# Decode attention with a gated MLP on one core: three adjoining slabs, wq in one transfer, wo in fewer, x and gate turned on VectorE

## The chip, the core and the metric

The kernel runs on one core of a Trainium2 chip. A core has a matrix engine (TensorE, "PE" in the profile, its weight loads "PEld"), VectorE ("DVE"), ScalarE ("ACT"), GpSimd ("POOL") and SyncE ("SP"), which here does nothing but issue transfers from the chip's memory into the on-chip buffer and back. The engines run side by side and wait for one another through semaphores. 16 DMA engines carry the transfers. The metric is the device time of one execution in microseconds; the kernel before takes 696.23 us (median of 3 runs, 696.22 to 696.31).

## The reference

Two tokens (batch B = 2, one position) of width 640. One branch is an attention block over a cache of 4096 positions with 32 heads of 128, the other a small MLP; a sigmoid gate mixes them.

```
g = sigmoid((x * gate_w).sum(-1, keepdims=True))            # x: (2, 1, 640)
q = (x @ wq).reshape(B, 1, 32, 128).transpose(0, 2, 1, 3)   # wq: (640, 4096)
scores = einsum("bhqd,bhkd->bhqk", q, k_cache) * 128 ** -0.5
o = einsum("bhqk,bhkd->bhqd", softmax(scores), v_cache)     # caches: (2, 32, 4096, 128)
a = o.transpose(0, 2, 1, 3).reshape(B, 1, 4096) @ wo        # wo: (4096, 640)
b = silu(x @ w1) @ w2                                       # w1: (640, 1728), w2: (1728, 640)
out = g * a + (1 - g) * b
```

All is float32. The two caches are 268 MB of the 298 MB that are read; wq and wo are 10.5 MB each, w1 and w2 4.4 MB each.

## The kernel before

**Tiling.** An item is four heads of one batch row; there are 16 (`items`, N = 16). For one item K is one contiguous run of 8.4 MB, loaded as 128 partitions of 16384 elements into a slab, and V likewise. There are three slabs, `slab_a`, `slab_b` and `slab_v`: K alternates between a and b, V uses v, except V of the last item, which goes into a.

**One item.** TensorE spreads the item's query over the partitions (`query`), GpSimd and VectorE multiply K by it (`products`), VectorE sums over 128 elements (`scores`) and finds the maximum (`peak`), ScalarE takes the exponentials (`weights`), TensorE multiplies them with V (`values`, 32 matmuls at L759), VectorE scales (`combine`), TensorE gathers (`gather`) and VectorE turns the result into columns of `oP` (`turn`).

**What sets the order.** The program is recorded once, operation by operation, in `Flow`: every `f.op` and `f.dma` names what it reads and writes, and `plan` works out the waits. Each engine then runs its list in the order of recording. All loads are issued by SP in order, so a load that waits holds up every load behind it in SP's list. Once issued, transfers of the one queue follow one another on the DMA engines. A slab's next load waits for the users of the slab: K of item i + 2 for `scores` of item i, V of item i + 1 for `values` of item i.

**The start.** SP issues w1 (into part of slab v), x (two rows) and gate (one row) beside it, wq in two pieces (8.4 MB into slab a, 2.1 MB into slab v), w2 into slab b, and a first write of zeros to the output. TensorE turns x and gate with matmuls against the identity (`mm_xT`), VectorE copies them (`xz`, `gx`), and the gate's sum goes through TensorE, ScalarE and VectorE to g and 1 - g (`gc`). `mm_qr` forms the queries of all heads in two PSUM banks, its first 32 matmuls from slab a, its last 8 from slab v; the load of the first K into slab a stands between them in the recording. ScalarE copies the queries out (`copy_qr`); a shifted identity brings the second batch row to where the first stood. `mm_hr` forms the hidden layer of the MLP from w1, VectorE rearranges it (`spaced`, `turned`, `he`, `seq`), and `ffn_out` (L587) multiplies by w2. The first V waits for `mm_hr`, the second K for `ffn_out`.

**The end.** After the last V, wo is loaded in four groups of 1024 rows (2.6 MB each; `load_wo`). Groups 0 and 1 are one transfer each and group 2 is two, all into slab v once the V before the last has been used; group 3 is three transfers of 5, 2 and 1 rows per partition into slab b. `in_halves` (L610) multiplies groups 0 to 2, eight steps each with two matmuls a step; for groups 0 and 1 the steps alternate between two halves of the output bank, for group 2 they stay in one. `merge` copies the bank and folds it with four matmuls (L627), `in_quarters` (L640) adds group 3 with four matmuls a step, VectorE copies the result, and SP sends it.

Of the kernel before, what the change touches and what calls it, by code (L numbers as in the profile page):

```python
# [16 lines left out]
class Flow:  # L17
# [22 lines left out]
    def op(self, eng, fn, reads=(), writes=(), by=(), signal=None, loop=None, after=(), lower=()):  # L40
        deps = list(after)
        for r in reads:
            if r in self.writer:
                deps.append(self.writer[r])
            if r.startswith("ps_"):
                deps += [d for d in self.readers.get(r, ()) if d.eng != eng]
        for w in writes:
            if w in self.writer:
                deps.append(self.writer[w])
            deps += self.readers.get(w, ())  # L50
        o = Op(eng, fn, deps, by, signal, loop)
        o.dma, o.lower = False, lower
        o.idx = len(self.ops[eng])
        self.ops[eng].append(o)
# [19 lines left out]
    def plan(self):  # L74
        seen = {e: {} for e in self.engines}
        for o in self.all:
# [88 lines left out]
def gated_decode(nc, x, kc, vc, wq, wo, w1, w2, gate, out):  # L165
    P = 128
# [46 lines left out]
    IW = 160  # L213
    ident_w = sb("ident", [P, IW])
    ident = ident_w[:, :P]
    ones = sb("ones", [P, P])
    fold = sb("fold", [P, 2 * Q, Q, 4])
    sel = sb("sel", [P, 4 * Q])
# [6 lines left out]
    g = sb("g", [P, B])  # L225
    gc = sb("gc", [P, B])
    ge = sb("ge", [P, B])
    gx = sb("gx", [P, B, J])
# [60 lines left out]
    def load_wo(g):  # L289

        n, at = ("v", g * PD) if g < NP - 1 else ("b", 0)
        src = wo[g * PR * P : (g + 1) * PR * P, :].rearrange("(p n) d -> p (n d)", n=PR)
        cuts = (0, PD) if g < NP - 2 else (0, PD // 2, PD) if g < NP - 1 else (0, FIRST * D, PD - D, PD)
        after = f.users(part(n)) if g in (0, NP - 1) else wo_after
        for k, (c0, c1) in enumerate(zip(cuts, cuts[1:])):
            f.dma("SP", slab[n][:, at + c0 : at + c1], src[:, c0:c1], writes=part(n, g % (NP - 1) + k), after=after)
        return after

    wq_rows = wq.rearrange("(p j) n -> p (j n)", j=J)
    f.dma(
        "SP",
        slab["v"][:, W1_AT : W1_AT + J * F],
        w1.rearrange("(p j) f -> p (j f)", j=J),
        writes=part("v", 1, 2, 3, 4, 5),
    )
    xg = slab["v"][: B + 1, XG_AT : XG_AT + D]
    f.dma("SP", xg[:B], x.rearrange("b s d -> (b s) d"), writes=part("v", 6))
    f.dma("SP", xg[B : B + 1], gate[None, :], writes=part("v", 7))  # L310
    f.dma("SP", slab["a"], wq_rows[:, :SLAB], writes=part("a"))
    f.dma("SP", slab["v"][:, :W1_AT], wq_rows[:, SLAB:], writes=part("v", 0))
    f.dma(
        "SP",
        slab["b"][:, : FH * HD],
        w2.rearrange("(p r) (e c) -> p (r e c)", p=P // 2, e=2).rearrange("p (e c) -> (p e) c", e=2),
        writes=part("b"),
    )

    f.op("POOL", lambda: G_.memset(ident_w, 0.0), writes=["ident"])  # L320
    f.op(
        "POOL",
        lambda: G_.affine_select(
# [15 lines left out]
    for q in range(Q):  # L339
# [38 lines left out]
        reads=["ident"],  # L378
        writes=["side"],
    )  # L380
    for q in range(Q):
        f.op(
            "DVE",
            lambda q=q: V.tensor_copy(
                spread[:, q * QP : (q + 1) * QP], ident[:, 32 * q : 32 * q + 1].to_broadcast([P, QP])
            ),
            reads=["ident"],
            writes=[f"spread{q}"],
        )
    SPREAD = [f"spread{q}" for q in range(Q)]  # L390
# [18 lines left out]

    def mm_xT():
        for j in range(J):
            last = T_.matmul(
                ps_v[:, j * (B + 1) : (j + 1) * (B + 1)],
                xg[:, j:D:J],
                ident[: B + 1, : B + 1],
                start=True,
                stop=True,
            )  # L420
        return last

    f.op("PE", mm_xT, reads=part("v", 6, 7) + ["ident"], writes=["ps_v"])
    xT = ps_v[:, : J * (B + 1)].rearrange("p (j r) -> p j r", j=J)
    f.op("DVE", lambda: V.tensor_copy(xz[:, :, :B], xT[:, :, :B]), reads=["ps_v"], writes=["xz"])
    for b in range(B):
        f.op(
            "DVE",
            lambda b=b: V.tensor_mul(gx[:, b, :], xT[:, :, B], xz[:, :, b]),
            reads=["ps_v", "xz"],  # L430
            writes=[f"gx{b}"],
        )
    f.op("DVE", lambda: V.reduce_sum(gp, gx, axis=AX.X), reads=["gx0", "gx1"], writes=["gp"])
    f.op(
        "PE",
        lambda: T_.matmul(ps_o[:, :B], ones, gp, start=True, stop=True),
# [15 lines left out]
    qr = (ps_0, ps_1)  # L452
    HALF = HQ // 2

    def mm_qr(j0, j1):
        for j in range(j0, j1):
            t, k = (slab["a"], j) if j < J0 else (slab["v"], j - J0)
            w = t[:, k * H * DH : (k + 1) * H * DH].rearrange("p (h q d) -> p h q d", q=Q, d=DH)
# [11 lines left out]
    f.op("PE", lambda: mm_qr(0, J0), reads=part("a") + ["xz"], writes=["ps_0", "ps_1"])  # L470
    load_k(0)
    f.op("PE", lambda: mm_qr(J0, J), reads=part("v", 0) + ["xz"], writes=["ps_0", "ps_1"])

    def copy_qr(u, b):
        return S_.copy(qall[:, u * HALF : (u + 1) * HALF, b, :], qr[u].rearrange("p (h d) -> p h d", d=DH))

    for u in range(2):
        f.op("ACT", lambda u=u: copy_qr(u, 0), reads=[f"ps_{u}"], writes=[f"qall{u}0"])

    def mm_query(i):  # L480
        return T_.matmul(  # L481
# [22 lines left out]

    query(0)
    copy_q(0)
    for u in range(2):
        f.op(
            "PE",
            lambda u=u: T_.matmul(  # L510
                qr[u],
                ident_w[:, 1 : P + 1],
                qall[:, u * HALF : (u + 1) * HALF, 0, :],
                start=True,
                stop=True,
            ),
            reads=["ident", f"qall{u}0"],
            writes=[f"ps_{u}"],
        )
        f.op("ACT", lambda u=u: copy_qr(u, 1), reads=[f"ps_{u}"], writes=[f"qall{u}1"])  # L520

    rows = ps_v
    w1t = slab["v"][:, W1_AT : W1_AT + J * F].rearrange("p (j f) -> p j f", j=J)

    def mm_hr():
        for j in range(J):
            for c in range(Q):
                last = T_.matmul(  # L530
                    rows[32 * c : 32 * c + 32, :QF],
                    xz[:, j, :],
                    w1t[:, j, c * QF : (c + 1) * QF],
                    start=(j == 0),
                    stop=(j == J - 1),
                )
        return last

    f.op("PE", mm_hr, reads=part("v", 1, 2, 3, 4, 5) + ["xz"], writes=["ps_v"])


    tv = turned[:, : 32 * FR].rearrange("p (n r) -> p n r", r=32)
    h = tv[:, :, :B]
    pairs = rows[:, :QF].rearrange("p (m s) -> p s m", s=FH)
    for e in range(2):
        f.op(
# [22 lines left out]
            writes=[f"seq{e}"],  # L569
        )  # L570

    load_v(0)

# [5 lines left out]
    def ffn_out(n):  # L579
# [13 lines left out]
                )  # L593
            return last

        f.op("PE", fn, reads=["seq0", "seq1"] + part(n), writes=["ps_acc"])

    def heads(g):
        return [f"oP{g}{u}{b}" for u in range(2) for b in range(B)]
# [1 line left out]
    def in_halves(g):  # L601

        for k in range(PR):
# [12 lines left out]
                    )  # L616
                return last

            f.op("PE", fn, reads=part("v", g + (g == NP - 2 and k >= PR // 2)) + heads(g), writes=["ps_acc"])

    def merge():
        f.op("ACT", lambda: S_.copy(partial, early), reads=["ps_acc"], writes=["partial"])
# [223 lines left out]
    for i in range(N + 1):  # L846
# [20 lines left out]
            peak(i)  # L867
            weights(i)
        if i == N - 1:
            wo_after = None  # L870
            for g_ in range(NP):
                wo_after = load_wo(g_)
        if j >= 0:
            combine(j)
            gather(j, by=by("combine"), loop=loop)
# [71 lines left out]
```

## Time and profile before

| | |
|---|---|
| median of 3 runs | 696.23 us (696.22 to 696.31) |
| profiled execution | 696.23 us |
| its span in the profile | 694.9 us |
| bytes read | 298.26 MB |
| DVE busy | 488.7 us (70% of the span) |
| POOL busy | 266.0 us (38%) |
| PE busy | 219.6 us (32%) |
| granted TensorE clock, mean | 0.67 |

How to read the profile's lines. A timeline row is: start in us, duration, engine, source line, operation, output<-input, shape, how many instructions were merged into the row, and in brackets how long the engine had been idle before it and what ended that idle time. A row of the chain gives start, duration and what ran. A row of groups gives count, busy time, mean ns of one, and the idle time before with what ended it. A row of transfers gives the count, the size and the time from issue to landing. A row of windows gives the stretch, its length, the busy time of each engine in it (PE, PEld, DVE, ACT, POOL, each with its number of instructions), the granted TensorE clock, the share of the DMA engines and the rate in GB/s; asked for PE alone, it has the columns of PE only. "SPq" is SyncE issuing a transfer. TensorE leaves two records for one float32 matmul.

### The profile page before, as it was taken

The page shows a single profiled execution, that of the slowest core. Times are in us where ns is not written, and L with a number is a line of the kernel's source. Part 1 is how long each engine was busy: PE and PEld are TensorE (multiplying, and loading weights), DVE is VectorE, ACT ScalarE, POOL GpSimd, SP SyncE. Part 2 cuts the span into 40 slices and gives each one's busy share as a digit, 9 for nine tenths or more (in the row PEclk, how much of TensorE's full clock was granted, in tenths as well). Part 3 has the DMA queues.
Part 4 walks back from the last instruction along what each step waited for, and adds up shares of the span by engine and source line. Part 5 has one row for each costly group of instructions (what it writes and reads, how often), then busy time and mean ns, then how long its engine had stood idle before and what let it go on. Part 6 is the DMA issues. An engine that isn't in the chain of part 4 may idle for free. (4 is left out here: it accounts for less than half of the span.)

```text
span 694.9 us, 3685 instructions
## 1 busy us (share of the span) xinstructions
PE 219.6 (32%) x1478; PEld 73.6 (11%) x1478; DVE 488.7 (70%) x263; ACT 41.2 (6%) x153; POOL 266.0 (38%) x26
## 2 busy tenths in 40 slices
PE   1095032151331406060412405060503214050657
PEld 1022010010110102020100101010101001010113
DVE  2001958898989596886959595987869595978811
ACT  0010010101010102010010101010010101010100
POOL 1000808191826080816335170907244260908100
PEclk9998556565575757575665757575665757575789
DMA  9999999999999999999999999999999999999997
GB/s 378 427 458 438 438 423 426 426 456 438 423 430 426 453 438 426 430 423 456 434 430 430 423 453 438 430 430 423 449 438 434 430 423 434 449 438 426 426 417 310
DMA packets 6229, 298.37 MB, mean 429 GB/s; under 512 B 699, under 2 KB 715, under 8 KB 974
## 3 DMA queue, kind: packets, MB, share of 16 engines
q1 hardware_dynamic: 6222, 298.28, 99.3%
q8 instruction: 4, 0.07, 0.0%
q14 instruction: 3, 0.02, 0.0%
HBM read 298.26 MB, written 0.01 MB: 429 GB/s over the span
## 5 line engine op out<-in xcount | busy, mean ns | idle before, releaser
L759 PE MATMUL ps<-slab_v,pz 128*32 128x512 f32 x960 | 139.3, 745 | 334.4 <-PEq L151 334.4
L663 POOL TENSOR_TENSOR slab_a<-slab_a,qsb 128x7680 f32<-128x7680 f32 x8 | 131.5, 16436 | 207.0 <-DMA slab_a<-in_A_k_cache_dram 191.9
L663 POOL TENSOR_TENSOR slab_b<-slab_b,qsb 128x7680 f32<-128x7680 f32 x8 | 131.4, 16428 | 171.4 <-DMA slab_b<-in_A_k_cache_dram 155.5
L679 DVE TENSOR_REDUCE s<-slab_a 128x68 f32<-128x8704 f32 (+1 forms) x16 | 138.2, 8676 | 0.0
L679 DVE TENSOR_REDUCE s<-slab_b 128x68 f32<-128x8704 f32 (+1 forms) x16 | 138.2, 8676 | 0.0
L669 DVE TENSOR_TENSOR slab_b<-slab_b,ps 128x8704 f32<-128x8704 f32 x8 | 73.8, 9219 | 48.0 <-DMA slab_b<-in_A_k_cache_dram 48.0
L669 DVE TENSOR_TENSOR slab_a<-slab_a,ps 128x8704 f32<-128x8704 f32 x8 | 73.8, 9219 | 43.5 <-DMA slab_a<-in_A_k_cache_dram 43.5
L759 PEld LDWEIGHTS ps<-slab_v,pz 128*32 128x32 f32 x960 | 37.7, 133 | 423.6 <-issue 423.6
L708 ACT ACTIVATE pz<-s,nb 32x128 f32<-32x128 f32 x64 | 25.5, 398 | 563.9 <-PE ps L759 361.5
L797 PE MATMUL ps<-osb,pick 128*128 128x512 f32 x32 | 20.4, 724 | 60.8 <-PEq L151 59.8
L781 DVE SCALAR_TENSOR_TENSOR osb<-ps,rg,own 128x512 f32<-128x512 f32 x16 | 12.0, 749 | 23.9 <-PE ps L759 23.9
L811 DVE TENSOR_REDUCE row<-ps 64x128 f32<-64x512 f32 x16 | 10.9, 683 | 23.3 <-PE ps L797 23.3
L548 DVE COPY spaced<-ps 128x224 f32<-128x224 f32 x2 | 0.7, 386 | 33.1 <-PE ps L530 33.1
L481 PE MATMUL ps<-qall,spread 128*128 (+1 forms) x32 | 7.4, 319 | 31.8 <-PEq L151 31.1
L461 PE MATMUL ps<-slab_a,xz 128*32 128x512 f32 x64 | 9.3, 747 | 16.1 <-DMA slab_a<-in_A_wq_dram 16.1
L797 PEld LDWEIGHTS ps<-osb,pick 128*128 128x128 f32 x32 | 5.4, 211 | 74.8 <-issue 73.0
L708 ACT ACTIVATION_READ_ACCUMULATOR pz<-s,nb 32x1 f32 x64 | 11.8, 184 | 0.0
L481 PEld LDWEIGHTS ps<-qall,spread 128*128 128x128 f32 x32 | 6.7, 224 | 41.9 <-issue 40.3
L759 PE MATMUL ps<-slab_a,pz 128*32 128x512 f32 x64 | 8.4, 687 | 7.1 <-DMA slab_a<-in_A_v_cache_dram 7.1
L818 DVE STREAM_TRANSPOSE ps<-row 64x256 f32<-64x256 f32 x16 | 10.3, 643 | 0.6
L587 PE MATMUL ps<-slab_b,seq 128*32 128x320 f32 x54 | 9.4, 505 | 3.0 <-DVE seq L565 3.0
L610 PE MATMUL ps<-slab_v,oP 128*32 128x320 f32 x96 | 9.2, 434 | 1.6 <-DMA slab_v<-in_A_wo_dram 1.6
(70 smaller groups left out, 92.0 us busy)
## 6 DMA issues: line engine op xcount, KB each, us to landing
slab_v<-in_A_wo_dram SPq DMA_DIRECT2D x2, 2560.0 KB, 18.5
slab_v<-in_B_w_dram SPq DMA_DIRECT2D x1, 4320.0 KB, 14.0
slab_b<-in_B_w_dram SPq DMA_DIRECT2D x1, 4320.0 KB, 46.3
slab_v<-in_A_wo_dram SPq DMA_DIRECT2D x2, 1280.0 KB, 25.9
slab_v<-in_A_wq_dram SPq DMA_DIRECT2D x1, 2048.0 KB, 36.6
slab_b<-in_A_wo_dram SPq DMA_DIRECT2D x1, 1600.0 KB, 30.5
slab_b<-in_A_wo_dram SPq DMA_DIRECT2D x1, 640.0 KB, 31.6
slab_b<-in_A_wo_dram SPq DMA_DIRECT2D x1, 320.0 KB, 31.9
```

What stands on the lines that cost most here:

```text
L461: last = T_.matmul(qr[u][32 * q : 32 * q + 32, :], xz[:, j, :], w[:, u * HALF : (u + 1) * HALF, q, :], start=(j == 0), stop=(j == J - 1),)
L481: return T_.matmul(ps_q[:, :DH], spread, qall.rearrange("p h b d -> p (h b) d")[:, i, :], start=True, stop=True,)
L587: last = T_.matmul(early[to : to + 32, :], seq[:, k : k + 2, :].rearrange("p k z -> p (k z)"), slab[n][:, k * HD : (k + 1) * HD], start=(k ...
L663: lambda: G_.tensor_mul(k[:, CV:, :], k[:, CV:, :], qsb[:, None, :].to_broadcast([P, C - CV, DH])),
L669: lambda: V.tensor_mul(k[:, :CV, :], k[:, :CV, :], ps_q[:, None, :DH].to_broadcast([P, CV, DH])),
L679: lambda c0=c0, c1=c1: V.reduce_sum(Ss[i % 2][:, c0:c1], k[:, c0:c1, :], axis=AX.X),
L708: last = S_.activation(pz[lo:hi, :, 4 * q : 4 * q + 4], s[lo:hi].rearrange("p (g c) -> p g c", c=4), AF.Exp, bias=nb[lo:hi], scale=SCALE, ...
L759: last = T_.matmul(ps_v[32 * q : 32 * q + 32, :], pz[:, gr, :], v[:, gr, :], start=(gr < 4), stop=(gr >= NG - 4),)
L781: lambda: V.scalar_tensor_tensor(osb, ps_v.rearrange("p (c d) -> p c d", d=DH), rg, own[:, :, None].to_broadcast([P, 4, DH]), op0=ALU.mult ...
L797: lambda *_: T_.matmul(ps_o, pick, osb.rearrange("p c d -> p (c d)"), start=True, stop=True),
L811: lambda: V.reduce_sum(row, ps_o[:64].rearrange("p (c d) -> p d c", d=DH), axis=AX.X),
L818: lambda: V.transpose(oT.rearrange("p n (e i) -> p n e i", e=2), twice),
```

## The change

- The three slabs become one tensor `slabs` with three adjoining parts, in the order v, b, a. wq (20480 elements per partition) is one transfer that covers slab b and the end of slab v; `mm_qr` is one run of 40 matmuls. w1 moves to slab a and w2 to the start of slab v.
- The load of the first K into slab a is recorded after `mm_hr`, which now comes before `mm_qr`. The first V is recorded after `ffn_out`, whose weights lie in slab v.
- x and gate are loaded as twelve pieces of 160 elements onto partitions of a zeroed tile `xs` (8 of x, 4 of gate), and VectorE turns them in 32 x 32 blocks; `mm_xT` goes away.
- The queries are copied out by VectorE with a 0/1 mask per batch row (four operations), in place of ScalarE's four copies and the shifted identity's two matmuls. `spread` is built by memsets.
- wo: groups 0 and 1 in one transfer, group 2 in one. Group 3 stays at three.
- `plan` sorts the waits by the order of recording.

```diff
-            for d in sorted(o.deps, key=lambda d: -d.idx):
+            for d in sorted(o.deps, key=lambda d: -d.turn):
...
-    slab = {n: sb(f"slab_{n}", [P, SLAB], 512) for n in "abv"}
+    slabs = sb("slabs", [P, 3 * SLAB], 512)
+    slab = {n: slabs[:, k * SLAB : (k + 1) * SLAB] for k, n in enumerate("vba")}
...
+    xs = turned[:, : D // Q]
+    xt = sb("xt", [P, J, 32])
+    mask = sb("mask", [P, B])
...
-    J0 = SLAB // (H * DH)
-    W1_AT = (J - J0) * H * DH
-    XG_AT = W1_AT + J * F
+    WQ_AT = 2 * SLAB - J * H * DH
...
         n, at = ("v", g * PD) if g < NP - 1 else ("b", 0)
+        if g == 0:
+            src = wo[: 2 * PR * P, :].rearrange("(g p n) d -> p g (n d)", g=2, n=PR)
+            to = slab["v"][:, : 2 * PD].rearrange("p (g c) -> p g c", g=2)
+            f.dma("SP", to, src, writes=part("v", 0, 1), after=v_users)
+            return
+        if g == 1:
+            return
         src = wo[g * PR * P : (g + 1) * PR * P, :].rearrange("(p n) d -> p (n d)", n=PR)
-        cuts = (0, PD) if g < NP - 2 else (0, PD // 2, PD) if g < NP - 1 else (0, FIRST * D, PD - D, PD)
-        after = f.users(part(n)) if g in (0, NP - 1) else wo_after
+        cuts = (0, PD) if g < NP - 1 else (0, FIRST * D, PD - D, PD)
+        after = f.users(part(n)) if g == NP - 1 else v_users
...
+    f.op("POOL", lambda: G_.memset(xs, 0.0), writes=["xs"])
+    f.dma("SP", slab["a"][:, : J * F], w1.rearrange("(p j) f -> p (j f)", j=J), writes=part("a"))
+    f.dma("SP", xs[0:P:HB, :], x.rearrange("b s (c n) -> (s c) b n", c=Q), reads=["xs"], writes=["xs0"])
+    f.dma("SP", xs[HB // 2 : P : 32, :], gate.rearrange("(c n) -> c n", c=Q), reads=["xs"], writes=["xs1"])
+    f.dma("SP", slabs[:, WQ_AT : 2 * SLAB], wq.rearrange("(p j) n -> p (j n)", j=J), writes=part("v", 1) + part("b"))
     f.dma(
         "SP",
-        slab["b"][:, : FH * HD],
+        slab["v"][:, : FH * HD],
         w2.rearrange("(p r) (e c) -> p (r e c)", p=P // 2, e=2).rearrange("p (e c) -> (p e) c", e=2),
-        writes=part("b"),
+        writes=part("v", 0),
     )
...
+        lambda: V.transpose(xt, xs.rearrange("p (n j) -> p j n", j=J)),
+        reads=["xs0", "xs1"],
...
+    f.op("PE", mm_hr, reads=part("a") + ["xz"], writes=["ps_v"])
+
+
+    load_k(0)
...
+    f.op("PE", mm_qr, reads=part("v", 1) + part("b") + ["xz"], writes=["ps_0", "ps_1"])
+    for u in range(2):
+        for b in range(B):
+            f.op(
+                "DVE",
+                lambda u=u, b=b: V.tensor_scalar(
+                    qall[:, u * HALF : (u + 1) * HALF, b, :],
+                    qr[u].rearrange("p (h d) -> p h d", d=DH),
+                    mask[:, b : b + 1],
+                    None,
+                    op0=ALU.mult,
+                ),
...
-            f.op("PE", fn, reads=part("v", g + (g == NP - 2 and k >= PR // 2)) + heads(g), writes=["ps_acc"])
+            f.op("PE", fn, reads=part("v", g) + heads(g), writes=["ps_acc"])
...
-    ffn_out("b")
+    ffn_out("v")
+    load_v(0)
     load_k(1)
```

On SP, the end of the list before (the transfers of wo, right after the last V's):

```order
L68 DMA slab_v<-in_A_wo_dram 128x5120 [waits done_PE]
L68 DMA slab_v<-in_A_wo_dram 128x5120
L68 DMA slab_v<-in_A_wo_dram 128x2560 x2
L68 DMA slab_b<-in_A_wo_dram 128x3200 [waits done_DVE]
L68 DMA slab_b<-in_A_wo_dram 128x1280
L68 DMA slab_b<-in_A_wo_dram 128x640
```

and after:

```order
L69 DMA slabs<-in_A_wo_dram 128x2x5120 [waits done_PE]
L69 DMA slabs<-in_A_wo_dram 128x5120
L69 DMA slabs<-in_A_wo_dram 128x3200 [waits done_DVE]
L69 DMA slabs<-in_A_wo_dram 128x1280
L69 DMA slabs<-in_A_wo_dram 128x640
```

Seven transfers become five; the last three are as they were.

On PE, the start of the list before:

```order
L414 MATMUL ps<-ident,slab_v 128x3 x5
L436 MATMUL ps<-gp,ones 128x2
L461 MATMUL ps<-slab_a,xz 32x512 x32
L461 MATMUL ps<-slab_v,xz 32x512 x8
L481 MATMUL ps<-qall,spread 128x128
...
L510 MATMUL ps<-qall,ident 128x512 x2
L530 MATMUL ps<-slab_v,xz 32x432 x20
L587 MATMUL ps<-slab_b,seq 32x320 x27
```

and after:

```order
L436 MATMUL ps<-slabs,xz 32x432 x20
L451 MATMUL ps<-gp,ones 128x2
L476 MATMUL ps<-slabs,xz 32x512 x40
L502 MATMUL ps<-qall,spread 128x128
L572 MATMUL ps<-slabs,seq 32x320 x27
```

The MLP's first matmuls (L530 before, L436 after) moved ahead of the queries' (L461 before, L476 after), and the five of `mm_xT` and two of the shifted identity are gone.

More of the change, by code (lines that the diff above doesn't have):

```diff
@@ L53, in op @@
         o.idx = len(self.ops[eng])
+        o.turn = len(self.all)
         self.ops[eng].append(o)
@@ L320, in gated_decode @@
-    f.op("POOL", lambda: G_.memset(ident_w, 0.0), writes=["ident"])
+        slab["v"][:, : FH * HD],
+        w2.rearrange("(p r) (e c) -> p (r e c)", p=P // 2, e=2).rearrange("p (e c) -> (p e) c", e=2),
+        writes=part("v", 0),
+    )
+    f.op("POOL", lambda: G_.memset(ident, 0.0), writes=["ident"])
     f.op(
@@ L380, in gated_decode @@
     )
+    f.op("DVE", lambda: V.memset(spread, 0.0), writes=["spread"])
     for q in range(Q):
@@ L453, in gated_decode, with mm_qr @@
     HALF = HQ // 2
[L455 to L458, printed above, removed]
+    def mm_qr():
+        for j in range(J):
+            at = WQ_AT + j * H * DH
+            w = slabs[:, at : at + H * DH].rearrange("p (h q d) -> p h q d", q=Q, d=DH)
             for u in range(2):
@@ L468, in mm_qr @@
         return last
[L470 to L475, printed above, removed]
-    for u in range(2):
-        f.op("ACT", lambda u=u: copy_qr(u, 0), reads=[f"ps_{u}"], writes=[f"qall{u}0"])
+    f.op("PE", mm_qr, reads=part("v", 1) + part("b") + ["xz"], writes=["ps_0", "ps_1"])
+    for u in range(2):
+        for b in range(B):
+            f.op(
+                "DVE",
+                lambda u=u, b=b: V.tensor_scalar(
[5 more added lines that the diff above has]
+                ),
+                reads=[f"ps_{u}", "mask"],
+                writes=[f"qall{u}{b}"],
+            )
     def mm_query(i):
@@ L506, in gated_decode @@
     copy_q(0)
[L507 to L539, printed above, removed]
     tv = turned[:, : 32 * FR].rearrange("p (n r) -> p n r", r=32)
-    h = tv[:, :, :B]
+    h = tv[:, :, ::HB]
     pairs = rows[:, :QF].rearrange("p (m s) -> p s m", s=FH)
@@ L570, in gated_decode @@
         )
-    load_v(0)
     def ffn_out(n):
```

81 lines of the change are left out of this document (35 added, 46 removed).

## The prediction

> **What bounds the kernel now.** I read the page from the top: shares of the engines, the slices, the queues; then the chain that ended last; then the timeline of the first 70 and the last 20 us, since the change edits only these two.
>
> ```profile
> PE 219.6 (32%) x1478; PEld 73.6 (11%) x1478; DVE 488.7 (70%) x263; ACT 41.2 (6%) x153; POOL 266.0 (38%) x26
> DMA  9999999999999999999999999999999999999997
> q1 hardware_dynamic: 6222, 298.28, 99.3%
> HBM read 298.26 MB, written 0.01 MB: 429 GB/s over the span
> ```
>
> No compute engine is near full, and the one DMA queue fills 99.3% of the span (690.0 of 694.9 us). The change moves the same bytes, so what it can win is what lies outside that 99.3%: 4.9 us, at the two ends. What it can lose is larger: any moment at which the queue runs dry, and any compute that is put behind the last transfer. The chain says what stands there today.
>
> ```profile
> 659.47 30.55 DMA slab_b<-in_A_wo_dram
> 690.02 0.14 issue
> 690.15 2.16 PE ps L640 x56
> ...
> 692.34 0.51 PE ps L640 x8
> ...
> 692.88 0.33 DVE slab_v L884
> ```
>
> The end is a transfer (the first piece of wo's fourth group, group 3 in the code), then the 32 matmuls of `in_quarters` on it, the copy, and the output's transfer up to 694.9. The profiled execution took 696.23 us, 1.33 outside its span, and is equal to the median of the three runs, so the sum below is made on 696.23 directly. The timeline shows what the tensor engine does before that.
>
> ```profile
> 677.76 4.51 PE L610 MATMUL ps<-slab_v,oP 128*32 128x320 f32 x64
> 683.23 2.35 PE L610 MATMUL ps<-slab_v,oP 128*32 128x320 f32 x16 [0.95 <-DMA slab_v<-in_A_wo_dram]
> 686.27 2.35 PE L610 MATMUL ps<-slab_v,oP 128*32 128x320 f32 x16 [0.69 <-DMA slab_v<-in_A_wo_dram]
> 688.66 0.42 ACT L622 COPY slab_v<-ps 128x320 f32<-128x320 f32 x1 [28.92 <-PE ps L610]
> 689.14 0.47 PE L627 MATMUL ps<-slab_v,join 128*17 128x160 f32 x8 [0.53 <-ACT slab_v L622]
> 690.15 2.66 PE L640 MATMUL ps<-slab_b,oP 128*17 128x160 f32 x64 [0.55 <-DMA slab_b<-in_A_wo_dram]
> ```
>
> Each matmul leaves two records. Groups 0 and 1 (four blocks of output rows) take 4.51 us for 64 records; group 2 (two blocks) takes 2.35 us for 16, twice, and its first half is done while the second half is still on its way. That overlap is what one transfer for group 2 takes away.
>
> **The tail, the term that I expect to decide.** On SP and PE the third group becomes one piece. PE before:
>
> ```order
> L610 MATMUL ps<-slab_v,oP 32x320 [waits load_434]
> L610 MATMUL ps<-slab_v,oP 32x320 x15
> L610 MATMUL ps<-slab_v,oP 32x320 [waits load_435]
> L610 MATMUL ps<-slab_v,oP 32x320 x7
> L610 MATMUL ps<-slab_v,oP 32x320 [waits load_436]
> L610 MATMUL ps<-slab_v,oP 32x320 x7
> ```
>
> PE after, same place (the end of the output projection; load_431 is groups 0 and 1, load_432 group 2, load_433 the first piece of group 3):
>
> ```order
> L595 MATMUL ps<-slabs,oP 32x320 [waits load_431]
> L595 MATMUL ps<-slabs,oP 32x320 x31
> L595 MATMUL ps<-slabs,oP 32x320 [waits load_432]
> L595 MATMUL ps<-slabs,oP 32x320 x15
> L612 MATMUL ps<-slabs,join 17x160 [waits done_ACT]
> L612 MATMUL ps<-slabs,join 17x160 x3
> L625 MATMUL ps<-slabs,oP 17x160 [waits load_433,done_DVE]
> ```
>
> All 16 matmuls of group 2 now stand behind the landing that the second eight waited for, and groups 0 and 1 behind the landing of group 1. The latter is hidden: the burst from 677.76 met no wait at its middle, so group 1 had landed by 680.0, and 4.51 us from there end at 684.5, before group 2 lands. For group 2 I need the pace inside a burst and the pace of the quarters:
>
> ```profile
> 687.64 0.12 PEld L610 LDWEIGHTS ps<-slab_v,oP 128*32 128x32 f32 x2 [0.15 <-issue]
> 687.91 0.12 PEld L610 LDWEIGHTS ps<-slab_v,oP 128*32 128x32 f32 x2 [0.15 <-issue]
> 690.12 1.25 PEld L640 LDWEIGHTS ps<-slab_b,oP 128*17 128x17 f32 x40 [0.85 <-issue]
> 691.57 0.40 PEld L640 LDWEIGHTS ps<-slab_b,oP 128*17 128x17 f32 x16 [0.20 <-DMA slab_b<-in_A_wo_dram]
> 692.34 0.13 PEld L640 LDWEIGHTS ps<-slab_b,oP 128*17 128x17 f32 x8 [0.36 <-DMA slab_b<-in_A_wo_dram]
> ```
>
> A pair of records follows the next after 0.27 us, so 8 more matmuls cost 8 x 0.27 = 2.16 and the burst 2.35 + 2.16 = 4.51 us (at most 2 x 2.35 = 4.70). It starts at 686.2 and ends at 690.7. The copy and the join follow as now: join starts 689.14 - 688.62 = 0.52 later, at 691.2, its own weights take about 0.13, so the quarters can issue from 691.35, at the latest after the join's 0.47, from 691.7. By then their data has landed but for the last pieces. Eight steps at 1.25/5 = 0.25 are 2.0, and the last record ends 692.85 - 692.47 = 0.38 behind the last weights: end between 693.7 and 694.1, against 692.85 now. Today the quarters wait for their pieces (the 0.20 and 0.36 above); then those waits are gone and PE itself is late. The term is +0.85 to +1.25; I take +0.9, near the lower end, since a weight load overlaps the matmul ahead of it in every row above.
>
> **What fewer transfers save.** The last three transfers tell a transfer's own cost.
>
> ```profile
> slab_b<-in_A_wo_dram SPq DMA_DIRECT2D x1, 1600.0 KB, 30.5
> slab_b<-in_A_wo_dram SPq DMA_DIRECT2D x1, 640.0 KB, 31.6
> slab_b<-in_A_wo_dram SPq DMA_DIRECT2D x1, 320.0 KB, 31.9
> 659.47 1.38 SPq L68 DMA_DIRECT2D slab_b<-in_A_wo_dram  x3
> ```
>
> They are issued 0.46 us apart, so 640 KB land 1.56 us after the first, and 320 KB 0.76 us later: twice 0.76 less 1.56 leaves -0.04 for a fixed cost, with rounding -0.2 to +0.2. Three transfers fewer (wq 1, wo 2) save between -0.6 and +0.6; I take 0, as calculated. The 640-byte pieces of x and gate carry 7.5 KB as before and lie inside w1's and wq's time; 0.
>
> The Trainium skill (DMA: Bandwidth & Descriptors, Rules for kernel authors) says to coalesce many small transfers, and its section on the anatomy of one DMA gives a fixed cost of about 2 us each on another issuing path; by that, an estimate of 3 x 2 = 6 us would be saved. The rows above do not agree: queued transfers hide it.
>
> **The start.** SP before, then after:
>
> ```order
> L68 DMA slab_a<-in_A_wq_dram 128x16384
> L68 DMA slab_v<-in_A_wq_dram 128x4096
> L68 DMA slab_b<-in_B_w_dram 128x8640
> L68 DMA out_dram<-oP 4x2x160 [waits done_POOL]
> L68 DMA slab_a<-in_A_k_cache_dram 128x16384 [waits done_PE,load_4]
> L68 DMA slab_v<-in_A_v_cache_dram 128x16384 [waits done_PE]
> L68 DMA slab_b<-in_A_k_cache_dram 128x16384 [waits done_PE]
> ```
>
> ```order
> L69 DMA slabs<-in_A_wq_dram 128x2x10240
> L69 DMA slabs<-in_B_w_dram 128x8640
> L69 DMA out_dram<-oP 4x2x160 [waits done_POOL]
> L69 DMA slabs<-in_A_k_cache_dram 128x16384 [waits done_PE]
> L69 DMA slabs<-in_A_v_cache_dram 128x16384 [waits done_PE]
> L69 DMA slabs<-in_A_k_cache_dram 128x16384
> ```
>
> The first K now waits only for the MLP's first matmuls (it can be issued well before 43.52, and queues behind w2 all the same: 0). The first V moves the other way: w2 lies in the v slab, so V waits for `ffn_out`, and `ffn_out` now stands behind all of wq and behind four masked copies on VectorE.
>
> ```profile
> slab_v<-in_A_wq_dram SPq DMA_DIRECT2D x1, 2048.0 KB, 36.6
> 2.24 0.53 SPq L68 DMA_DIRECT2D slab_v<-in_A_wq_dram  x1
> 34.06:45.11 11.05, 11.04 (x80) 2.73 (x80) 0.00 (x0) 0.00 (x0) 0.00 (x0) 1.00 1.04 447
> 51.86 0.69 DVE L548 COPY spaced<-ps 128x224 f32<-128x224 f32 x2 [33.11 <-PE ps L530]
> 54.78 9.42 PE L587 MATMUL ps<-slab_b,seq 128*32 128x320 f32 x54 [2.99 <-DVE seq L565]
> L781 DVE SCALAR_TENSOR_TENSOR osb<-ps,rg,own 128x512 f32<-128x512 f32 x16 | 12.0, 749 | 23.9 <-PE ps L759 23.9
> 43.52 0.33 SPq L68 DMA_DIRECT2D slab_a<-in_A_k_cache_dram  x1
> 51.85 0.33 SPq L68 DMA_DIRECT2D slab_v<-in_A_v_cache_dram  x1
> slab_a<-in_A_k_cache_dram SPq DMA_DIRECT2D x1, 24.8
> 693.23 0.55 SPq L68 DMA_DIRECT2D out_dram<-slab_v  x1
> ```
>
> wq has landed at 2.24 + 36.6 = 38.84. Its 40 matmuls took 11.05 us (some of it early, on the first piece; now all of it after): 50.0. The four copies have no row; one lies between 0.35 (224 elements, L548) and 0.75 (512 elements with more operands, L781); I take 0.65, nearer the one of equal size: 52.6. From the spacing copies to `ffn_out` 54.78 - 51.86 = 2.92: 55.5. `ffn_out` 9.42: V is issued at about 65.0 instead of 51.85 (63.8 to 65.4 with the copies' bounds). The first K lands at 43.52 + 24.8 = 68.3; from an issue to the end of a small transfer it is at most 694.9 - 693.23 = 1.7, so V must be issued by 66.6. Margin 1.6 us: I cost it at 0, but the cover is thin, and was 14.7 us. The second K follows at once and has a whole V in hand (8.4 MB at 429 GB/s, 19.5 us). Every other edit of the start (the POOL memset ahead of x, x's turn and the gate on VectorE, the four matmuls and two ACT copies gone) lies under the transfers from w1 to the first K: 0. The points where the repeated and prefetched parts of the instruction lists are cut move by a few operations; VectorE waited 43.5 us for the K slabs of one of the two buffers alone, which covers it:
>
> ```profile
> L669 DVE TENSOR_TENSOR slab_a<-slab_a,ps 128x8704 f32<-128x8704 f32 x8 | 73.8, 9219 | 43.5 <-DMA slab_a<-in_A_k_cache_dram 43.5
> ```
>
> Sum: 696.23 + 0.9 + 0 + 0 = 697.1 us, 0.13% slower, which is inside the 0.2% (1.4 us) that a measurement of this kernel can about tell from no change.
>
> **Rivals.** First, slower: the clock falls in the tail. It fell once after a pause:
>
> ```profile
> 54.78:55.96 1.18, 1.18 (x8) 0.49 (x10) 0.00 (x0) 0.00 (x0) 0.00 (x0) 0.90 0.77 333
> 55.96:59.37 3.41, 3.41 (x16) 1.24 (x14) 0.00 (x0) 0.00 (x0) 0.00 (x0) 0.54 1.06 461
> ```
>
> The burst came after 2.99 us without work, and 1.2 us into it the granted clock went to 0.54 for 3.41 us. In the new tail PE pauses from 684.5 at the latest to 686.2, about 2 us, where it now pauses 0.95 and 0.69. If the clock falls there, 3.41 us run at half speed and cost 1.7: 698.8. Against it: the pause is shorter than the one that did it.
>
> The Trainium skill (TensorE: Matmul & The Clock Gate, Why this matters for your kernels) warns only of idle gaps over about 3 us; by it the sum stays as it is, and the trace's one drop agrees.
>
> Second, slower: V is issued later than 66.6. One more stretch of 3.41 us at half clock in wq's burst or in `ffn_out` costs 1.7, and the upper bound of the copies 0.4: V at 67.1, the queue stands still for 0.5, 697.6; a second such stretch makes it 699.3. It decides from 67.1 on. For it speaks that both bursts now begin after a longer pause than before.
>
> Third, no loss in the tail: the 16 DMA engines do not end together.
>
> ```profile
> 689.50:690.00 0.50, 0.10 (x4) 0.00 (x0) 0.00 (x0) 0.00 (x0) 0.00 (x0) 1.00 0.89 358
> 690.00:690.50 0.50, 0.35 (x12) 0.37 (x16) 0.00 (x0) 0.00 (x0) 0.00 (x0) 1.00 0.36 143
> ```
>
> From 690.0 only a third is busy: a few late engines set each landing. If the late ones are less late after the change, group 2 lands up to about 1.5 us sooner and all follows: 697.1 - 0.9 = 696.2 with a typical part of it.
>
> Fourth, faster: each transfer has a cost that the last pieces hide. At the 0.76 us of the whole smallest piece, three of them are 2.3: 697.1 - 2.3 = 694.8. This is the coalescing rule of the Trainium skill (DMA: Bandwidth & Descriptors, Rules for kernel authors) at a price from this trace.
>
> **Numbers.** Forecast 0.60, clock 0.13, late V 0.12, no loss 0.11, transfers' cost 0.04. Slower by over 0.2% is above 697.62: the clock (0.13), three quarters of the late V (0.09) and a tenth of the forecast (0.06): 0.28. Faster, below 694.84: most of the fourth, a little of the third: 0.04. The rest, 0.68, is no change. The range from 696.2 (third rival) to 698.5 (between the two prices of the late V, short of the clock's 698.8) leaves out 0.13 for the clock and a few hundredths each of the late V and the fourth, about 0.2.
>
> **What would show it.** Right: one burst of 32 records at L595 of about 4.5 us that starts near 686 and waits for wo; L625 without waits for its pieces, ending 0.8 to 1.2 us later than now; V's issue near 65; the queue still at 99%. Wrong: a granted clock near 0.5 after 684; no packets around 67 to 69; the first product on a K slab, right after the first K's landing, moved; or a middle of the run in which slabs wait differently.

## The result

The changed kernel takes 699.13 us (median of 6 runs, 698.76 to 699.43) against 696.23 us: a ratio of 1.0041, 95% interval 1.0031 to 1.0052. That is slower by 2.9 us; forecast were 697.1 and a range up to 698.5.

| | before | after |
|---|---|---|
| median | 696.23 us | 699.13 us |
| profiled execution | 696.23 us | 698.83 us |
| its span | 694.9 us | 696.6 us |
| spans of the other runs | 694.4 to 695.3 us (18 runs beside the first experiments) | 696.5 to 697.2 us |
| time outside the span (time less span, median over runs) | 1.34 us | 2.25 us |

Two things moved: the span by about 1.95 us (696.85 in the median of the runs, against 694.9) and the time outside it by 0.91. The queue is still full on the page of the profile after:

```profile
DMA  9999999999999999999999999999999999999996
q1 hardware_dynamic: 6060, 298.27, 99.1%
```

The chain that ended last, however, is another one.

```profile
659.39 27.35 DMA slabs<-in_A_wo_dram
...
686.79 4.53 PE ps L595 x32
...
691.34 0.43 ACT slabs L607
...
691.82 0.47 PE ps L612 x8
692.28 2.22 PE ps L625 x64
...
694.52 0.33 DVE slabs L870
```

It no longer ends in the transfer of the fourth group of wo but in that of the third: the burst of 32 records, the copy, the join and the quarters stand behind it one after the other. From that landing to the last matmul are 694.50 - 686.79 = 7.71 us; before they were 692.85 - 686.27 = 6.58. The burst also starts 0.52 us later than the second half of that group did (686.27).

The start, by the timeline of after:

```profile
38.87 11.09 PE L476 MATMUL ps<-slabs,xz 128*32 128x512 f32 x80 [17.13 <-DMA slabs<-in_A_wq_dram]
50.04 2.72 DVE L490 TENSOR_SCALAR qall<-ps,mask 128x512 f32<-128x512 f32 x4 [27.49 <-PE ps L476]
55.63 10.18 PE L572 MATMUL ps<-slabs,seq 128*32 128x320 f32 x54 [4.30 <-DVE seq L551]
65.84 0.33 SPq L69 DMA_DIRECT2D slabs<-in_A_v_cache_dram  x1
```

GpSimd's first product on a slab starts as soon as that K has landed, so its rows date the landings of the first and the second K. Before:

```profile
68.43 16.43 POOL L663 TENSOR_TENSOR slab_a<-slab_a,qsb 128x7680 f32<-128x7680 f32 x1 [64.57 <-DMA slab_a<-in_A_k_cache_dram]
107.27 16.42 POOL L663 TENSOR_TENSOR slab_b<-slab_b,qsb 128x7680 f32<-128x7680 f32 x1 [22.41 <-DMA slab_b<-in_A_k_cache_dram]
```

After:

```profile
68.49 16.43 POOL L649 TENSOR_TENSOR slabs<-slabs,qsb 128x7680 f32<-128x7680 f32 x1 [64.48 <-DMA slabs<-in_A_k_cache_dram]
108.44 16.44 POOL L649 TENSOR_TENSOR slabs<-slabs,qsb 128x7680 f32<-128x7680 f32 x1 [23.52 <-DMA slabs<-in_A_k_cache_dram]
```

The first K is on time, the second 1.17 us late: the loss lies between them, where the first V is transferred. The windows show it; before, then after. The last two columns are the DMA share and the rate; a packet counts in full in the window in which it starts, so a share can exceed 1. A row of K or V, 64 KB, is one packet.

```profile
63.90:65.75 1.85, 0.30 (x2) 0.00 (x0) 0.00 (x0) 0.00 (x0) 0.00 (x0) 1.00 1.23 531
65.75:66.75 1.00, 0.00 (x0) 0.00 (x0) 0.00 (x0) 0.00 (x0) 0.00 (x0) 1.00 1.37 590
66.75:68.25 1.50, 0.00 (x0) 0.00 (x0) 0.00 (x0) 0.00 (x0) 0.00 (x0) 1.00 0.71 306
68.25:69.75 1.50, 0.00 (x0) 0.00 (x0) 1.37 (x1) 0.00 (x0) 1.32 (x1) 0.87 1.31 568
```

```profile
63.90:65.75 1.85, 1.85 (x14) 0.56 (x8) 0.00 (x0) 0.00 (x0) 0.00 (x0) 1.00 1.31 567
65.75:66.75 1.00, 0.06 (x1) 0.00 (x0) 0.00 (x0) 0.00 (x0) 0.00 (x0) 1.00 0.00 0
66.75:68.25 1.50, 0.00 (x0) 0.00 (x0) 0.00 (x0) 0.00 (x0) 0.00 (x0) 1.00 2.01 699
68.25:69.75 1.50, 0.00 (x0) 0.00 (x0) 1.38 (x1) 0.00 (x0) 1.26 (x1) 1.00 0.00 0
69.75:71.25 1.50, 0.00 (x0) 0.00 (x0) 1.50 (x1) 0.00 (x0) 1.50 (x1) 0.87 1.61 699
```

Before, the engines took up new rows all along. After, they took up K's last sixteen rows from 63.9 us on, at 2.4 us a row (1.31 x 1.85), so the first of them were free from about 66.3; but not one row started between 65.75 and 66.75. Then V's first sixteen rows started (699 GB/s over 1.5 us are 1.05 MB), and they took 3.0 us each on average (2.01 x 1.5), where the next sixteen took 2.4 (1.61 x 1.5). So the engines that were free first stood still for some 0.4 us, and the slower first rows added 0.6: an estimate of 1.0 of the 1.17 us.

Last, what the DMA engines do at the very end (694 to 700 us). After, a transfer of the kind that the profile calls "instruction" stands there, behind the span's end (an instruction load, for short):

```profile
q14 instruction: 1, 0.01, 0.5%
q1 hardware_dynamic: 12, 0.01, 0.3%
```

Before, only the output:

```profile
q1 hardware_dynamic: 12, 0.01, 0.3%
```

So there were three candidates: the late V, the longer chain at the end, and something outside the span. The experiments take them one at a time, first by undoing each in the changed kernel, then by putting each alone into the kernel before.

### The profile page after: what moved, and what is told of

It reads as the page before. It is cut to its first block, busy times and chain, and to the rows that moved or that the text cites. A ratio compares the mean times of both kernels' runs of the same rounds, so it can differ in the third digit from the quotient of the medians.

```text
span 696.6 us, 3657 instructions
## 1 busy us (share of the span) xinstructions
PE 215.6 (31%) x1464; PEld 71.1 (10%) x1464; DVE 492.1 (71%) x269; ACT 39.0 (6%) x149; POOL 266.4 (38%) x27
## 5 line engine op out<-in xcount | busy, mean ns | idle before, releaser
L649 POOL TENSOR_TENSOR slabs<-slabs,qsb 128x7680 f32<-128x7680 f32 x16 | 263.2, 16448 | 379.2 <-DMA slabs<-in_A_k_cache_dram 348.2
L665 DVE TENSOR_REDUCE s<-slabs 128x68 f32<-128x8704 f32 (+1 forms) x32 | 276.3, 8676 | 0.0
L745 PE MATMUL ps<-slabs,pz 128*32 128x512 f32 x1024 | 145.8, 733 | 341.8 <-PEq L152 334.8
L655 DVE TENSOR_TENSOR slabs<-slabs,ps 128x8704 f32<-128x8704 f32 x16 | 147.5, 9219 | 93.4 <-DMA slabs<-in_A_k_cache_dram 93.4
L745 PEld LDWEIGHTS ps<-slabs,pz 128*32 128x32 f32 x1024 | 39.6, 132 | 434.8 <-issue 427.7
L476 PE MATMUL ps<-slabs,xz 128*32 128x512 f32 x80 | 11.1, 720 | 17.1 <-DMA slabs<-in_A_wq_dram 17.1
L572 PE MATMUL ps<-slabs,seq 128*32 128x320 f32 x54 | 10.2, 539 | 4.3 <-DVE seq L551 4.3
L436 PE MATMUL ps<-slabs,xz 128*32 128x432 f32 x40 | 5.8, 749 | 15.6 <-DVE xz L422 15.6
L595 PE MATMUL ps<-slabs,oP 128*32 128x320 f32 x96 | 9.0, 434 | 3.1 <-DMA slabs<-in_A_wo_dram 3.1
L719 PE MATMUL ps<-rs,fold 128*128 128x1 f32 x32 | 6.1, 260 | 3.5 <-PEq L152 3.4
```

The source lines that it names most:

```text
L476: last = T_.matmul(qr[u][32 * q : 32 * q + 32, :], xz[:, j, :], w[:, u * HALF : (u + 1) * HALF, q, :], start=(j == 0), stop=(j == J - 1),)
L595: last = T_.matmul(early[to + 32 * n : to + 32 * n + 32, :], oP[:, at : at + 32], slab["v"][:, s_ * D + n * W2 : s_ * D + (n + 1) * W2], s ...
L649: lambda: G_.tensor_mul(k[:, CV:, :], k[:, CV:, :], qsb[:, None, :].to_broadcast([P, C - CV, DH])),
L655: lambda: V.tensor_mul(k[:, :CV, :], k[:, :CV, :], ps_q[:, None, :DH].to_broadcast([P, CV, DH])),
L665: lambda c0=c0, c1=c1: V.reduce_sum(Ss[i % 2][:, c0:c1], k[:, c0:c1, :], axis=AX.X),
L745: last = T_.matmul(ps_v[32 * q : 32 * q + 32, :], pz[:, gr, :], v[:, gr, :], start=(gr < 4), stop=(gr >= NG - 4),)
```

## The experiments

The first four experiments ran on one chip, the next four on a second and the last four on a third, each with runs of the kernel before beside them (medians 696.15, 695.86 and 695.82 us, spans 694.8, 694.5 and 694.5), so each is compared with those. The changed kernel's own span, 696.85, is from the result above.

**wo as before, in the changed kernel.** The merged load of groups 0 and 1 is taken out again, and group 2 is cut:

```diff
-        if g == 0:
-            src = wo[: 2 * PR * P, :].rearrange("(g p n) d -> p g (n d)", g=2, n=PR)
...
-        cuts = (0, PD) if g < NP - 1 else (0, FIRST * D, PD - D, PD)
+        cuts = (0, PD) if g < NP - 2 else (0, PD // 2, PD) if g < NP - 1 else (0, FIRST * D, PD - D, PD)
...
-            f.op("PE", fn, reads=part("v", g) + heads(g), writes=["ps_acc"])
+            f.op("PE", fn, reads=part("v", g + (g == NP - 2 and k >= PR // 2)) + heads(g), writes=["ps_acc"])
```

> The changed kernel with wo's seven transfers as before (groups 0 and 1 apart, group 2 in two pieces with its matmuls split in two). Theory: the burst of 32 records behind one landing costs 1.1 us at the end (from the landing of group 2 to the last matmul 7.67 us now, 6.58 before), so the span falls by 1.1 (696.6 to 695.5) and the first products on the second K slab still start at 108.4 (before: 107.3). Rival: the tail is late only because V was late at the start, then the span stays at 696.6. The time outside the span (2.23 us now, 1.33 before) falls too if the length of SP's list sets it, and stays otherwise.

Measured: 698.45 us (1.0031, 1.0019 to 1.0043). The median span is 695.75, so 1.1 less than in the changed kernel, as the theory said; outside the span stay 2.26 us, so SP's list does not set that. The profiled execution itself had a span of 697.5, because in it V was issued later still (the granted clock was 0.52 from 55 to 61 us there), and this gives a second dose of the late V:

```profile
66.94 0.33 SPq L69 DMA_DIRECT2D slabs<-in_A_v_cache_dram  x1
```

```profile
109.73 16.43 POOL L642 TENSOR_TENSOR slabs<-slabs,qsb 128x7680 f32<-128x7680 f32 x1 [24.65 <-DMA slabs<-in_A_k_cache_dram]
```

V 1.10 us later (66.94 for 65.84), the second K 1.29 us later (109.73 for 108.44): once the queue is dry, further delay is lost in full.

**The MLP first, in the changed kernel.** The VectorE chain to `seq` is recorded right after the gate, and the matmuls on w2 ahead of the first query:

```diff
     f.op("PE", mm_qr, reads=part("v", 1) + part("b") + ["xz"], writes=["ps_0", "ps_1"])
+    ffn_out("v")
+    load_v(0)
...
-    ffn_out("v")
-    load_v(0)
     load_k(1)
```

> The changed kernel with the MLP's VectorE chain ahead of the query copies and the matmuls on w2 ahead of the first query, so that the first V is issued near 59 us instead of 65.84. Theory: at 65.84 the DMA queue had run dry, and all later transfers are 1.15 us late; then the second K's products start at 107.3 (108.4 now), and the span is 1.1 shorter (695.5). Rival: the 1.15 us comes from wq's or w2's transfer, or from the longer instruction list; then the second K stays at 108.4 and the span at 696.6.

Measured: 698.25 us (1.0039, 1.0025 to 1.0053); median span 696.0, 0.85 less than in the changed kernel. Three of the five spans are 695.7 to 696.0, two are 697.6 and 697.9; the two were not profiled (a run with the same whole group 2, further down, shows a drop of the clock in such a case). The profile:

```profile
57.02 0.33 SPq L69 DMA_DIRECT2D slabs<-in_A_v_cache_dram  x1
```

```profile
107.26 16.46 POOL L644 TENSOR_TENSOR slabs<-slabs,qsb 128x7680 f32<-128x7680 f32 x1 [22.23 <-DMA slabs<-in_A_k_cache_dram]
```

The second K is back at 107.26. That settles the late V as the cause of its delay: wq and w2 are transferred as in the changed kernel. Of the 1.17 us at the second K, 0.85 comes back at the end.

**The zeroing on VectorE, in the changed kernel.**

```diff
-    f.op("POOL", lambda: G_.memset(xs, 0.0), writes=["xs"])
+    f.op("DVE", lambda: V.memset(xs, 0.0), writes=["xs"])
```

> The changed kernel with the zeroing of x's tile on VectorE instead of GpSimd, so that GpSimd has as many operations as before. Theory that GpSimd's list sets the 0.9 us outside the span: the time falls from 699.1 to 698.2 with the span as it is (696.6 to 697.2). Rival (another engine's list, or none): time and span both as in the changed kernel.

Measured: 698.09 us (1.0031, 1.0021 to 1.0041); span 696.7 in the median, as in the changed kernel, and 1.39 us outside it. One memset moved from GpSimd to VectorE takes back 0.9 us that no row of the span shows. The instruction load at the end is gone, too; the DMA engines from 694 us on:

```profile
q1 hardware_dynamic: 12, 0.01, 0.3%
```

**Early V and group 2 in two pieces, in the changed kernel** (the second run's edit, and of the first run's that on `cuts` and the waits of the matmuls).

> The changed kernel with both repairs: the MLP first (early V) and group 2 of wo in two pieces; groups 0 and 1 stay in one transfer. If the two losses are separate they add: span 696.6 - 1.15 - 1.1 = 694.4, and 695.7 to 696.6 in time, depending on what lies outside the span. If they are one and the same loss, the span is 695.5.

Measured: 697.37 us (1.0017, 1.0007 to 1.0027); median span 694.8 (694.4 to 695.1), 2.30 outside. Against 696.85 the two repairs give 2.05, and singly they gave 0.85 and 1.1: two separate losses. The merged load of groups 0 and 1, which stayed in, costs nothing and saves nothing. In three of the nine runs the time outside the span was 3.1 to 3.75 us, and in one of the first run's six 3.66 (five runs of the last two versions of the changed kernel below had 1.5 to 2.4); what stands behind that is open.

**One more GpSimd operation, in the kernel before.**

```diff
+    pad = sb("pad", [P, 8])
+    f.op("POOL", lambda: G_.memset(pad[:, 0:8], 0.0), writes=["pad0"])
     f.op("POOL", lambda: G_.memset(ident_w, 0.0), writes=["ident"])
```

> The kernel before with one more GpSimd operation, a memset of 8 elements on a tile of its own, at the head of GpSimd's list. Theory: the length of GpSimd's list sets the time outside the span; then time minus span goes from 1.3 to 2.2 us and the time to 697.1, with the span as before (694.9). Rival: it is the wait for the zeroed tile that cost it in the changed kernel, not the length; then 696.2 and 1.3.

Measured: 696.80 us against 695.86 (1.0013, 1.0004 to 1.0022); span 694.4 as before (694.5), 2.33 outside for 1.34. Nobody waits for that tile, so it is the length of the list. And the instruction load stands behind the span's end (694.3) again:

```profile
q14 instruction: 1, 0.01, 0.5%
```

**Group 2 whole, in the kernel before.**

```diff
-        cuts = (0, PD) if g < NP - 2 else (0, PD // 2, PD) if g < NP - 1 else (0, FIRST * D, PD - D, PD)
+        cuts = (0, PD) if g < NP - 1 else (0, FIRST * D, PD - D, PD)
...
-            f.op("PE", fn, reads=part("v", g + (g == NP - 2 and k >= PR // 2)) + heads(g), writes=["ps_acc"])
+            f.op("PE", fn, reads=part("v", g) + heads(g), writes=["ps_acc"])
```

> The kernel before with wo's third group in one transfer and its 16 matmuls behind one wait, nothing else. Theory: +1.1 us from the landing of that group to the last matmul (7.7 us for 6.6), span 696.0, time 697.2, 1.3 outside the span. Rival: the transfers behind it hide it, 696.2.

Measured: 697.79 us (1.0025, 1.0015 to 1.0036), 1.34 outside the span. The spans fall into two groups: 695.5 to 696.0 (four runs; 1.0 to 1.5 over the 694.5 of before) and 697.0 to 697.7 (four). The profiled execution is of the second; its timeline of PE, and the windows of PE on it:

```profile
686.22 6.19 PE L610 MATMUL ps<-slab_v,oP 128*32 128x320 f32 x32 [2.70 <-DMA slab_v<-in_A_wo_dram]
```

```profile
683.50:686.20 2.70, 0.02 (x3) 1.00 1.03 440
686.20:689.60 3.40, 3.38 (x14) 0.51 0.94 394
689.60:692.40 2.80, 2.80 (x22) 0.98 0.22 88
```

The burst takes 6.19 us, where it took 4.53 in the changed kernel, since the granted clock is 0.51 through its first 3.4 us, after a pause of 2.70 us. So the whole group costs 1.1 us and, in a part of the runs, 1.7 more. That the other three long runs are clock drops too is inferred from their spans; they were not profiled.

**V late, in the kernel before.** The first V is recorded behind `ffn_out` and waits for it:

```diff
-    def load_v(i):
+    def load_v(i, after=()):
...
-    load_v(0)
...
     ffn_out("b")
+    load_v(0, after=f.readers["b.0"][-1:])
     load_k(1)
```

> The kernel before with the first V issued after the matmuls on w2 (about 64.2 us) in place of 51.85, nothing else. By the two runs of the changed kind (issue 65.84 gives the second K's products at 108.4, issue 66.94 at 109.7) the loss begins near an issue at 64.8; so at 64.2 nothing is lost: the products start at 107.3, span 694.9, time 696.2. Rival: any issue later than the forecast lead of 1.7 us before K's end is free, also nothing lost here; another rival: the loss comes from two loads issued back to back, then 108.4 and 696.8.

Measured: 696.09 us (1.0009, 1.0000 to 1.0018). The profiled execution:

```profile
63.24 0.33 SPq L68 DMA_DIRECT2D slab_v<-in_A_v_cache_dram  x1
```

```profile
107.23 16.42 POOL L663 TENSOR_TENSOR slab_b<-slab_b,qsb 128x7680 f32<-128x7680 f32 x1 [22.55 <-DMA slab_b<-in_A_k_cache_dram]
```

An issue at 63.24 loses nothing, also with the second K issued right behind it (63.61). Four of the 11 runs have spans of 695.4 to 696.7; where V came in those is not known, but the issue hangs on PE's bursts, whose clock varies. The limit lies between 63.2 and 65.8 us. No run shows where: a straight line through the two doses gives 64.8; the first engine free at 66.3, less the 0.9 us from V's issue (65.84) to the first row (66.75 at the earliest), gives 65.4. Both are estimates.

**All three repairs, in the changed kernel** (the edits of the second, third and fourth run together).

> The changed kernel with all three repairs: MLP first (early V), group 2 of wo in two pieces, zeroing on VectorE. If the three losses are all there is, the span is 694.5 to 695.1 as with the first two, 1.35 outside it, and the time 695.9 to 696.4, the same as before (696.15). Rival: something else of the change costs, then above 696.7.

Measured: 695.97 us against 695.86 (1.0001, 0.9992 to 1.0010); span 694.5 (before 694.5), outside 1.36. With these three put right no loss is left beyond the interval (0.1% is 0.7 us), and nothing is gained either.

**The repairs, and GpSimd's list four shorter** (the memsets of xz, pz, oP and seq on VectorE too).

```diff
...
-    f.op("POOL", lambda: G_.memset(pz, 0.0), writes=["pz"])
...
+    f.op("DVE", lambda: V.memset(pz, 0.0), writes=["pz"])
...
```

> The changed kernel with the three repairs and GpSimd's other four memsets moved to VectorE too, so that GpSimd's list has four operations fewer than before. If the time outside the span follows the length of the list step by step it falls by 0.9 for each, or at all below 1.3, and this beats both kernels (695.0 or less); if the list only must not pass a limit, it stays at 1.35 and the time at 696.0.

Measured: 695.91 us against 695.82 (1.0001, 0.9992 to 1.0010), 1.32 outside. No version here beats the kernel before.

**Three more GpSimd operations, and one fewer, in the kernel before.**

```diff
+    pad = sb("pad", [P, 24])
+    f.op("POOL", lambda: G_.memset(pad[:, 0:8], 0.0), writes=["pad0"])
+    f.op("POOL", lambda: G_.memset(pad[:, 8:16], 0.0), writes=["pad1"])
+    f.op("POOL", lambda: G_.memset(pad[:, 16:24], 0.0), writes=["pad2"])
```

> The kernel before with three more GpSimd memsets of 8 elements. One more gave time minus span 2.3 us for 1.35. If a limit was passed, three more give the same 2.3 and 696.8; if each operation costs, 2.3 + 2 x 0.95 = 4.2 and 698.7.

```diff
-    f.op("POOL", lambda: G_.memset(seq, 0.0), writes=["seq"])
+    f.op("DVE", lambda: V.memset(seq, 0.0), writes=["seq"])
```

> The kernel before with one GpSimd memset (of seq) moved to VectorE, so that GpSimd's list is one shorter. A limit just above the list of before: nothing changes, 1.35 outside the span and 695.9. A cost per operation: 0.4 outside the span and 695.0.

Measured: 696.73 us with three more (1.0013, 1.0004 to 1.0023; 2.22 outside), 695.82 with one fewer (1.0000, 0.9990 to 1.0009; 1.32 outside). It is a step, not a slope, and the list of before stood at most one operation under it. The DMA engines from 694 us on with three more:

```profile
q14 instruction: 1, 0.01, 0.6%
```

**Group 2 whole on four blocks, in the kernel before.** On top of the edit with group 2 whole:

```diff
-    PACED = (NP - 2) * PR
+    PACED = (NP - 1) * PR
...
-                        stop=(s_ in (PACED - 1, PACED + PR - 1)),
+                        stop=(s_ in (PACED - 2, PACED - 1)),
```

> The kernel before with wo's third group in one transfer, as in the run with that change alone, but its steps alternating between the two halves of the bank like those of groups 0 and 1 (four blocks of output rows). Theory: the loss is the pace of the burst behind the landing; at the pace of groups 0 and 1 (16 steps in 4.51 us) eight steps take 2.4 us instead of 4.50, so the loss of 1.1 goes: span 694.5, time 695.9. It also ends the runs in which the clock fell (span 697 and more), or makes them cost little, since PE then waits for group 3 anyway. Rival: a later landing of the whole group costs, then 696.8 to 697.8 as there.

Measured: 696.39 us against 695.82 (1.0006, 0.9997 to 1.0015); spans 694.6 to 695.3, but 696.3 in the profiled execution. Most of the loss goes: 0.5 us in the median of the spans is left of 1.1 and more. The profiled execution shows the clock again, now after a pause of 3.10 us:

```profile
686.13 4.50 PE L610 MATMUL ps<-slab_v,oP 128*32 128x320 f32 x32 [3.10 <-DMA slab_v<-in_A_wo_dram]
```

```profile
685.60:689.00 3.40, 2.87 (x24) 0.50 1.00 422
689.00:692.00 3.00, 2.46 (x32) 0.51 0.45 180
```

At half clock the burst takes as long as the two-block burst at full clock. What the remaining 0.5 us of the other runs is stays open; none of those was profiled.

## Why the prediction was wrong, point by point

**What bounds the kernel.** Right for the span: the DMA queue, and only its two ends and a dry moment moved it. What lies outside the span it left out.

**The tail.** Right in mechanism, and the size lay inside its bounds. The forecast had the burst at 4.51 us, the join's start 0.52 us behind it and the end 0.85 to 1.25 us later; measured are 4.53, 691.82 - 691.32 = 0.50, and 7.71 - 6.58 = 1.13 us from the landing on. Undoing it gave 1.1 (first run). The value taken, 0.9, was 0.2 low.

**What fewer transfers save.** Right: 0. The changed kernel with the repairs still has wq in one transfer and groups 0 and 1 in one, and it equals the kernel before. That is two transfers fewer, at 695.97 against 695.86 us; the fourth rival's 0.76 us each would have made 1.5. So that rival falls, and with it the estimate from the Trainium skill's fixed cost of about 2 us (DMA: Bandwidth & Descriptors, Anatomy of one DMA — SWDGE (gpsimd) path): these queued transfers do not show it.

**The start: this step failed.** The issue of V was forecast at 65.0 and came at 65.84, inside the 66.6 that the prediction allowed. The copies took 2.72 us for 2.6 and the second burst 10.18 for 9.42, for its clock was at half for 5.17 us where before it was for 3.41:

```profile
55.63:60.80 5.17, 5.17 (x20) 1.85 (x22) 0.00 (x0) 0.00 (x0) 0.00 (x0) 0.52 0.99 431
```

The limit was wrong: "so V must be issued by 66.6. Margin 1.6 us: I cost it at 0". It took the end of K on the last DMA engine (68.3) and an upper bound of the latency (1.7 us, where the first row came 0.9 us or a little more behind the issue), and so asked when the last engine would idle. The queue pays as soon as the first engines run out, here from about 66.3, two us before the last; that early engines end well before the last the prediction itself had shown (its windows at 690 us). And the first rows after the pause took 3.0 us for 2.4. Measured: a limit between 63.2 and 65.8, and at 65.84 a loss of 1.17 us at the second K and 0.85 us at the end. The second rival named this mechanism, and the longer stretch of slow clock, but set its point at 67.1.

**What lies outside the span: this step failed too.** The sum was made "on 696.23 directly", with 1.33 us outside the span taken as fixed, and the added GpSimd memset was costed at 0 under the transfers. Its run time is hidden; its place in GpSimd's list is not. One operation more lifts the time outside from 1.34 to 2.33 us (in the kernel before), one fewer takes it back from 2.25 to 1.39 (in the changed kernel). No rival had it.

**The clock.** The first rival did not decide the changed kernel's profiled run: the burst took 4.53 us there. But it is real: 0.51 after a pause of 2.70 us with group 2 whole in the kernel before. The Trainium skill (TensorE: Matmul & The Clock Gate, Why this matters for your kernels) warns of idle gaps over about 3 us; this run does not agree with it as a safe limit. With group 2 whole, the profiled bursts behind pauses of 1.65, 1.68 and 2.11 us (the changed kernel, the third and the second run) kept the full clock; those behind 2.70 and 3.10 us did not.

**No loss in the tail** (third rival): the burst did start 0.52 us later rather than 1.17, so a part of the dry moment was made good by the end (that the engines that were late anyway lost less is argued, not shown); but the tail's own term came in full.

The sum, with the measured terms: 696.23 + 1.1 (tail) + 0.85 (V) + 0.91 (outside) = 699.09; measured 699.13. That it closes so well is partly luck, for single spans of one kernel differ by a few tenths of a us.

## What to carry to other kernels

Where one transfer queue is full for the whole run, ask of each edit how much lead every issue keeps before the first engine runs out of work, not the last; a lead that shrinks from 15 us to 1 us is a term with a price. Cutting the last large transfers finer lets compute start early, and merging them moves that compute behind the landing, where it costs time and may also meet a slow clock. And compare time with span: an operation that costs nothing in the span can still lengthen what lies behind it.

## What the runs showed of the hardware that was not expected

- Time outside the span is a step function of GpSimd's list: 1.32 to 1.39 us in the medians up to the length of before, 2.22 to 2.33 with one or three operations more. In the profiles of all 14 kernels, the six with the long time have an instruction load of 0.01 MB behind the span's end, and the eight with the short one have none. That this load is what costs the 0.9 us, and that it is GpSimd's, is argued from this and from GpSimd holding the last operation of the program; no row names its engine. The Trainium skill (Runtime: NRT & Kernel Launch, Instruction fetch mechanics) says that instructions come in blocks and that crossing into the next is mostly hidden; if this load is such a crossing, it is not hidden at the end of the program.
- A DMA queue that runs dry costs more than the gap: the first sixteen rows after it took 3.0 us each in place of 2.4, and a further 1.10 us of delay cost 1.29 us. Why those rows are slow is open.
- TensorE's granted clock fell to 0.51 after a pause of 2.70 us; in other runs of the same kernel it seems, by their spans, not to have fallen.
